# mLSTM into two gated layers, one core: set-up tiles, two-part gate rows and the order of VectorE at the start

## The chip, the cores and the metric

The program runs on one core of one Trainium2 chip. The time is device microseconds of that core, the median of three runs; "span" is the profiler's time from the first to the last instruction of one profiled execution. In the tables PE is TensorE, DVE is VectorE, ACT is ScalarE, POOL is GpSimd and SP is SyncE, whose queue issues every DMA here.

## What is computed

For 2 batches, 8 heads, 768 steps and a head size of 40, a recurrent attention with exponential gates, and then two dense layers with their own nonlinearities over the 1536 tokens of width 320:

```
m_new  = max(f + m, i);  f_stab = exp(f + m - m_new);  i_stab = exp(i - m_new)
C = f_stab*C + i_stab * v k^T;   n = f_stab*n + i_stab*k
y = sigmoid(o) * (C q) / max(|n.q|, 1)
x = y as [1536, 320]
x = (h - tanh h) @ w_out,            h = x @ w_in        (320 -> 2048 -> 320)
x = (h * tanh(softplus h)) @ w2_out, h = x @ w2_in       (320 -> 2048 -> 320)
```

## The kernel before

The recurrence is done in chunks of 128 steps. There are 12 token tiles (6 chunks of 2 batches); tile j is one `attention(j)`. The first dense layer takes tiles in blocks of two (`blk[0, k]`), so block 0 is tiles 0 and 1, and its 16 weight slices of 128 columns come in pairs: `mm1(i)` is the first product for a block and two slices, `tile1(i)` its nonlinearity, `mm2(i)` the second product. Every product that has to be precise is made from two fp32r parts, so x and each weight slice are first split in a high and a low part.

A weight slice (`conv_w`, line 166) is loaded raw and goes through three integer passes on VectorE with a scaling pass on ScalarE between the second and the third: L175, L176 (VectorE), L177 (ScalarE), L178 (VectorE, the third pass), then L179 (ScalarE, the high part) and L181 and L182 (the low part: GpSimd for the first two slices, VectorE for the others). The product `mm1(0)` needs slices 0 and 1 and x of tiles 0 and 1.

x of a tile is made at the end of `attention(j)`: products of q and k (L321), times the decay D on VectorE (L323), product with v on TensorE (L341), the denominator and two VectorE operations (L349 to L354) that write x, a copy (L141 from line 357). `transpose_x` turns it: TensorE L246, ScalarE L248 (high part), VectorE L249 (low part). D is an exponential of a sum that TensorE makes from the gate rows n and a; for chunk 0 from `n0` and `na` (L285 to L295), for later chunks from the tiles `md` and `sd` (L301), into whose rows DMAs (L269, L275) write the two-part rows `nr` of n and a.

`gates()` makes the gate rows: scans of chunk 0, their parts (`first` is the last of these, L418), and a closure `rest` that is called in steps: the scans over chunks 1 to 5 (L396 to L404), `rest_u` (L439 and the GpSimd operation L442), `rest_t` (an exponential L450, transposes and products on TensorE, the VectorE copies L454, L457 and L467) and `rest_n` (the two-part rows: two ScalarE copies L141 and two VectorE subtractions L435).

The tiles that GpSimd sets up are `cm` (L612, L613), `C` (L643), `sd` (L673, L674, L677) and `md` (L680, L683). `spin` (L592) are filler products on TensorE.

The order on each engine is made by a scheduler that takes instructions in the order in which they are traced when their inputs are expected to be ready. `after(x)` adds an edge: what is traced in it stands behind x in the queue of the engine that it shares with x. `start` holds the last instructions of `transpose_x` of tile 1 and the last L179; slices 2 and on are converted after it (`conv_to`).

## Time and profile before

| | us |
|---|---|
| runs before | 480.66, 477.70, 479.10 |
| median | 479.1 |
| profiled execution: its time | 479.02 |
| profiled execution: its span | 476.9 |
| TensorE busy in the span | 459.6 |
| VectorE, ScalarE, GpSimd busy | 320.7, 283.9, 119.5 |
| mean granted clock, share of full | 0.978 |

The profile was read on one core only, since there is one. Times of the timeline are from the span's start. A row of the timeline is: start, length, engine, line, operation, written<-read tiles, shapes, count, and in brackets the idle time of the engine just before and what ended it. Neighbouring rows of one engine may overlap by about 0.1 us, since an engine starts an instruction while the one before drains.

### The profile page before, as it was taken

To read this page: it belongs to the slowest core of one execution; us is meant where nothing else is said; L and a number is where in the kernel's file an instruction comes from. 1 tells how busy PE (TensorE), PEld (TensorE's weight loads), DVE (VectorE), ACT (ScalarE), POOL (GpSimd) and SP (SyncE) were. 2 spreads that over 40 slices of the span, in tenths; PEclk is the share of its full clock that TensorE was granted. 3 is DMA by queue.
4 is the path that set the end of the run, shared out by engine and by line. 5 is a ranking of instruction groups with operands and counts; after the bars stand their busy time and mean duration, and the time that the engine had idled before them with its cause. 6 is when DMAs were issued, how large, how long until landed. Compare 5 with 4: busy or idle time off the path is not lost.

```text
span 476.9 us, 8013 instructions
## 1 busy us (share of the span) xinstructions
PE 459.6 (96%) x3103; PEld 418.2 (88%) x3103; DVE 320.7 (67%) x544; ACT 283.9 (60%) x513; POOL 119.5 (25%) x132
## 2 busy tenths in 40 slices
PE   9868999999999999999999998999999999999996
PEld 5536898999999989999999887989989998998895
DVE  7889588998968888666899897789942321121111
ACT  3776837567576675797987675866744322332231
POOL 2912526427464252243332333100000000000000
PEclk9997959999999999999999999999999999999999
DMA  7954161542513321000101101055401000010001
GB/s 256 375 197 147 58 219 45 179 136 65 177 33 105 101 63 62 0 1 2 61 12 51 62 1 63 21 205 173 149 0 56 1 1 1 0 56 0 1 0 55
DMA packets 22745, 38.04 MB, mean 80 GB/s; under 512 B 1364, under 2 KB 17044, under 8 KB 22708
## 3 DMA queue, kind: packets, MB, share of 16 engines
q1 hardware_dynamic: 22708, 37.54, 23.8%
q8 instruction: 24, 0.39, 0.3%
q14 instruction: 13, 0.11, 0.1%
HBM read 35.41 MB, written 1.97 MB: 78 GB/s over the span
## 4 chain that ended last, share of the span: by engine, by line
PE 77%; DVE 8%; issue 5%; ACT 3%; DMA 3%; POOL 2%; ACTq 0%; DVEq 0%; POOLq 0%; SPq 0%
PE h L493 32%; PE acc L554 10%; PE acc L552 10%; PE acc L553 10%; PE sc L321 4%; PE pv L341 4%; DMA raw<-in_w_dram 3%; POOL gl L506 2%; PE it L330 2%; PE xt L246 1%; PE st L362 1%; DVE raw L176 1%; PE w_ps L592 1%; DVE g L522 1%; DVE raw L175 1%
## 5 line engine op out<-in xcount | busy, mean ns | idle before, releaser
L493 PE MATMUL h<-xT,w 128*128 128x256 f32 (+1 forms) x1152 | 212.3, 325 | 7.8 <-ACT w L179 3.4
L493 PEld LDWEIGHTS h<-xT,w 128*128 128x128 f32 x1152 | 170.8, 191 | 24.8 <-ACT w L179 4.0
L552 PE MATMUL acc<-w,gh 128*128 128x320 f32 x384 | 120.2, 315 | 1.3 <-ACT gh L141 0.8
L553 PE MATMUL acc<-w,gh 128*128 128x320 f32 x384 | 118.9, 312 | 0.0
L554 PE MATMUL acc<-w,gl 128*128 128x320 f32 x384 | 110.5, 312 | 0.1
L506 POOL TENSOR_TENSOR gl<-g,gh 128x512 fp32r<-128x512 f32 x48 | 66.5, 1386 | 137.9 <-ACT gh L141 124.0
L535 DVE TENSOR_TENSOR gl<-g,gh 128x512 fp32r<-128x512 f32 x48 | 33.1, 691 | 85.7 <-ACT g L534 85.7
L552 PEld LDWEIGHTS acc<-w,gh 128*128 128x128 f32 x384 | 73.0, 190 | 5.3 <-issue 1.3
L553 PEld LDWEIGHTS acc<-w,gh 128*128 128x128 f32 x384 | 72.8, 190 | 2.3
L533 ACT ACTIVATE gh<-h 128x512 fp32r<-128x512 f32 x48 | 28.8, 601 | 75.5 <-PE h L493 75.4
L554 PEld LDWEIGHTS acc<-w,gl 128*128 128x128 f32 x384 | 69.9, 189 | 1.8 <-POOL gl L506 0.3
L141 ACT ACTIVATE gh<-g 128x512 fp32r<-128x512 f32 x48 | 30.4, 634 | 29.8 <-DVE g L522 22.3
L522 DVE COPY_PREDICATED g<-u,t 128x512 f32<-128x512 uint32 x48 | 41.0, 855 | 7.5 <-ACT u L521 7.3
L519 DVE TENSOR_TENSOR g<-u,h 128x512 f32<-128x512 f32 x48 | 32.7, 681 | 14.7 <-ACT u L518 11.5
L521 ACT ACTIVATE u<-u,bias 128x512 f32<-128x512 f32 x48 | 34.9, 727 | 10.5 <-DVE g L519 10.4
L178 DVE SCALAR_TENSOR_TENSOR raw<-raw 128x704 uint32<-128x704 uint32 x32 | 34.5, 1082 | 7.5 <-ACT raw L177 7.3
L179 ACT ACTIVATE w<-raw 128x704 fp32r<-128x704 f32 x32 | 27.8, 875 | 16.0 <-DVE raw L178 15.9
L516 ACT ACTIVATE u<-h 128x512 f32<-128x512 f32 x48 | 28.4, 591 | 14.4 <-PE h L493 14.3
L177 ACT ACTIVATE raw<-raw 128x704 f32<-128x704 f32 x32 | 27.7, 867 | 9.3 <-DVE raw L176 8.3
L520 DVE TENSOR_TENSOR t<-h,t 128x512 f32<-128x512 f32 x48 | 32.8, 684 | 0.0
L176 DVE SCALAR_TENSOR_TENSOR raw<-raw 128x704 uint32<-128x704 uint32 x32 | 30.3, 948 | 0.3
L518 ACT ACTIVATE u<-u 128x512 f32<-128x512 f32 x48 | 30.5, 636 | 0.0
(105 smaller groups left out, 503.2 us busy)
## 6 DMA issues: line engine op xcount, KB each, us to landing
raw<-in_w_dram SPq DMA_DIRECT2D x32, 704.0 KB
qk_t<-in_qk_dram SPq DMA_DIRECT2D x12, 512.0 KB
kv_t<-in_kv_dram SPq DMA_DIRECT2D x12, 324.0 KB
out_dram<-xo SPq DMA_DIRECT2D x12, 160.0 KB
xo<-in_og_dram SPq DMA_DIRECT2D x2, 640.0 KB
xo<-in_og_dram SPq DMA_DIRECT2D x2, 320.0 KB
sd<-nr SPq DMA_DIRECT2D x20, 4.0 KB
md<-nr SPq DMA_DIRECT2D x10, 8.0 KB
```

The costliest lines, as they stand in the source:

```text
L176: nc.vector.scalar_tensor_tensor(lo32, in0=z, scalar=0x80000000, in1=lo32, op0=ALU.bitwise_and, op1=ALU.bitwise_or)
L178: nc.vector.scalar_tensor_tensor(z, in0=z, scalar=3, in1=lo32, op0=ALU.logical_shift_left, op1=ALU.bitwise_or)
L493: y = nc.tensor.matmul(t[:, k * nt:(k + 1) * nt], lhsT=w[:, o:o + P], rhs=x[:, kk, :], start=(n == 0), stop=(n == len(pairs) - 1),)
L506: nc.gpsimd.tensor_tensor(gl, in0=g, in1=gh.bitcast(F32), op=ALU.subtract)
L519: mark[:] = [nc.vector.tensor_tensor(g, in0=u, in1=h, op=ALU.mult)]
L520: nc.vector.tensor_tensor(t, in0=h, in1=t, op=ALU.subtract)
L521: nc.scalar.activation(out=u, in_=u, func=AF.Relu, bias=bias[:, 0:1])
L522: nc.vector.copy_predicated(out=g, mask=u.bitcast(U32), data=t)
L535: nc.vector.tensor_tensor(gl, in0=g, in1=gh.bitcast(F32), op=ALU.subtract)
L552: nc.tensor.matmul(a, lhsT=gh[:, sl], rhs=wh, start=(f in ends_), stop=False)
L553: nc.tensor.matmul(a, lhsT=gh[:, sl], rhs=wl, start=False, stop=False)
L554: nc.tensor.matmul(a, lhsT=gl[:, sl], rhs=wh, start=False, stop=(f + 1 in ends_ or f == NF - 1))
```

## The change

GpSimd's set-up of `sd`, `md` and `C` is traced right behind that of `cm` instead of behind the first two attentions, and the first row of `u_t` is cleared at the beginning. The steps of `rest` come in another order: the scans, `rest_n` and `rest_u` are called right after the first four steps of tile 0's attention; `rest_t` is now the one that is called after `start`. In `rest_n` the ScalarE copies stand behind the exponentials made so far, and the VectorE subtractions behind tile 0's last L323 (`scored[0]`); `rest_u`'s GpSimd operation stands behind the last `wv` (L316). For the first two weight slices the third pass (L178) of slice f stands behind the last operation on x of tile f (`gated[f]`, L354), and the first pass of slice 1 behind the third pass of slice 0.

```diff
@@ -128,6 +128,8 @@
     texp, tbl, dls = [], [], []
+    scored, gated = {}, {}
+
     spq, cvd, hold = [], [], []
     def after(x):
@@ -163,7 +165,9 @@
                     spq[:] = [x]
                 raw[layer, f] = t
-    def conv_w(layer, f):
+    third = {}
+
+    def conv_w(layer, f, first=(), behind=()):
         r = raw.pop((layer, f)).rearrange("p (n t) -> p n t", t=2)
         lo32, z = r[:, :, 0], r[:, :, 1]
         zf = z.bitcast(F32)
@@ -172,10 +176,14 @@
-        nc.vector.tensor_scalar(lo32, in0=lo32, scalar1=29, scalar2=None, op0=ALU.logical_shift_right)
+        with after(first):
+            nc.vector.tensor_scalar(lo32, in0=lo32, scalar1=29, scalar2=None, op0=ALU.logical_shift_right)
         nc.vector.scalar_tensor_tensor(lo32, in0=z, scalar=0x80000000, in1=lo32, op0=ALU.bitwise_and, op1=ALU.bitwise_or)
         scaled[layer, f] = nc.scalar.activation(out=zf, in_=zf, func=AF.Copy, scale=2.0 ** -111)
-        nc.vector.scalar_tensor_tensor(z, in0=z, scalar=3, in1=lo32, op0=ALU.logical_shift_left, op1=ALU.bitwise_or)
+        with after(behind):
+            third[layer, f] = nc.vector.scalar_tensor_tensor(
+                z, in0=z, scalar=3, in1=lo32, op0=ALU.logical_shift_left, op1=ALU.bitwise_or
+            )
         cvd[:] = [nc.scalar.activation(out=w[:, 0:WC], in_=zf, func=AF.Copy)]
         eng = nc.gpsimd if layer == 0 and f < PRE else nc.vector
         eng.tensor_tensor(w[:, WC:WT], in0=zf[:, 0:REM0], in1=wf[:, 0:REM0], op=ALU.subtract)
@@ -320,7 +328,7 @@
                 h = 4 * hf + hh
                 x = nc.tensor.matmul(sc[:, hh, :], lhsT=hp(kT, h, HP), rhs=hp(q, h, HP), start=True, stop=True)
             d4 = Dm[:, 4 * hf:4 * hf + 4, :]
-            nc.vector.tensor_tensor(d4, in0=sc, in1=d4, op=ALU.mult)
+            scored[j] = nc.vector.tensor_tensor(d4, in0=sc, in1=d4, op=ALU.mult)
             yield
         hv = ap_.tile([P, H, D1], F32, tag="hv", name="hv", bufs=2) if c else None
         hs = slice(b * H, (b + 1) * H)
@@ -351,7 +359,7 @@
         nc.vector.reciprocal(out=den, in_=den)
         x = xo[:, j, 0:DM].rearrange("p (h d) -> p h d", h=H)
         nc.vector.tensor_tensor(x, in0=hv[:, :, 0:D], in1=x, op=ALU.mult)
-        nc.vector.scalar_tensor_tensor(
+        gated[j] = nc.vector.scalar_tensor_tensor(
             x, in0=x, scalar=1 / WS, in1=den.to_broadcast([P, H, D]), op0=ALU.mult, op1=ALU.mult
         )
         copy_r(0, xo[:, j, DM:3 * P], xo[:, j, 2 * P:DM])
@@ -390,6 +398,7 @@
         nc.vector.memset(ch(rm)[:, :, 0:1], 0.0)
         nc.gpsimd.memset(na[0].bitcast(F32), 0.0)
         nc.gpsimd.memset(g_t, 0.0)
+        nc.gpsimd.memset(ch(u_t)[:, 0:1, :], 0.0)
         nc.gpsimd.tensor_tensor(sel, in0=ident[:, 0:BH], in1=ident[:, 32:32 + BH], op=ALU.add)
         def scans(a, e):
@@ -423,26 +432,29 @@
         first = parts(0)
         def rest():
-            nc.gpsimd.memset(ch(u_t)[:, 0:1, :], 0.0)
             with after([first]):
                 scans(L, S)
-            return rest_u
+            return rest_n
         def rest_n():
             for n, t in enumerate((n_t, i_t)):
                 t, hi, lo = t[:, EC * L:S], nr[64 * n:64 * n + BH], nr[64 * n + 32:64 * n + 32 + BH]
-                copy_r(0, hi, t)
-                nc.vector.tensor_tensor(lo, in0=t, in1=hi.bitcast(F32), op=ALU.subtract)
+                with after(texp):
+                    copy_r(0, hi, t)
+                with after([scored[0]]):
+                    nc.vector.tensor_tensor(lo, in0=t, in1=hi.bitcast(F32), op=ALU.subtract)
+            return rest_u
         def rest_u():
             mp = once.tile([BH, NCH, 1], F32, name="mp")
             nc.vector.tensor_tensor(
                 mp[:, 1:NCH, :], in0=ch(n_t)[:, 0:NCH - 1, L - 1:L], in1=ch(F_t)[:, 0:NCH - 1, L - 1:L], op=ALU.add
             )
-            dls[:] = [nc.gpsimd.tensor_tensor(
-                ch(u_t)[:, 1:NCH, :], in0=ch(n_t)[:, 1:NCH, :], in1=mp[:, 1:NCH, :].to_broadcast([BH, NCH - 1, L]),
-                op=ALU.subtract,
-            )]
+            with after(dls):
+                nc.gpsimd.tensor_tensor(
+                    ch(u_t)[:, 1:NCH, :], in0=ch(n_t)[:, 1:NCH, :], in1=mp[:, 1:NCH, :].to_broadcast([BH, NCH - 1, L]),
+                    op=ALU.subtract,
+                )
             return rest_t
         def rest_t():
@@ -465,7 +477,6 @@
                     rhs=ue.rearrange("p (b r g) c -> p r b g c", r=2, g=HG)[:, r], start=True, stop=True,
                 )
             nc.vector.tensor_copy(dec, d_ps)
-            return rest_n
         return rest, first
@@ -610,9 +621,31 @@
         big = cm.bitcast(F32)
         nc.gpsimd.memset(big, 0.0)
-        nc.gpsimd.affine_select(
+        masked = nc.gpsimd.affine_select(
             out=cm, in_=big, pattern=[[1, L]], base=0, channel_multiplier=-1, compare_op=ALU.is_ge, fill=2.0 ** 100
         )
+
+        for b, t in enumerate(sds):
+            f = t.bitcast(F32)
+            with after([masked]):
+                nc.gpsimd.memset(f, 0.0)
+            nc.gpsimd.affine_select(
+                out=t, in_=f, pattern=[[0, P]], base=-b, channel_multiplier=1, compare_op=ALU.not_equal, fill=1.0
+            )
+            nc.gpsimd.affine_select(
+                out=t, in_=f, pattern=[[0, P]], base=-B - b, channel_multiplier=1, compare_op=ALU.not_equal, fill=1.0
+            )
+        with after([masked]):
+            nc.gpsimd.memset(md_.bitcast(F32), 0.0)
+        mf = md_.bitcast(F32)
+        for n in range(2):
+            nc.gpsimd.affine_select(
+                out=md_, in_=mf, pattern=[[-HG, 2], [-1, HG], [0, L]], base=-K0 - H * n, channel_multiplier=1,
+                compare_op=ALU.not_equal, fill=-1.0,
+            )
+        with after([masked]):
+            for t in Cst:
+                nc.gpsimd.memset(t, 0.0)
         copy_r(0, identr, ident)
         for n, v_ in enumerate((-G_T,)):
             nc.vector.memset(bias[:, n:n + 1], v_)
@@ -634,13 +667,13 @@
                 next(g, 0)
         go(ga, 4)
+        rest = rest()
+        rest = rest()
+        rest = rest()
         go(gb, 4)
         session(0, 2)
         go(ga)
         go(gb)
-        with after(dls):
-            for t in Cst:
-                nc.gpsimd.memset(t, 0.0)
         go(ga)
         go(gb)
         loads_to(2 * B, "qk")
@@ -657,8 +690,11 @@
         def lead1(n, x=()):
             while conv1[0] < min(n, NF):
+                f = conv1[0]
                 with after(x):
-                    conv_w(0, conv1[0])
+                    conv_w(
+                        0, f, [third[0, f - 1]] if f and f < PRE else (), [gated[f]] if f < PRE else ()
+                    )
                 if conv1[0] >= PRE:
                     load_w()
                 if conv1[0] == PRE + 1:
@@ -666,29 +702,7 @@
                         load_o(*oc.pop(0))
                 conv1[0] += 1
-
-        with after(dls):
-            for b, t in enumerate(sds):
-                f = t.bitcast(F32)
-                nc.gpsimd.memset(f, 0.0)
-                nc.gpsimd.affine_select(
-                    out=t, in_=f, pattern=[[0, P]], base=-b, channel_multiplier=1, compare_op=ALU.not_equal, fill=1.0
-                )
-                nc.gpsimd.affine_select(
-                    out=t, in_=f, pattern=[[0, P]], base=-B - b, channel_multiplier=1, compare_op=ALU.not_equal, fill=1.0
-                )
-            nc.gpsimd.memset(md_.bitcast(F32), 0.0)
-            mf = md_.bitcast(F32)
-            for n in range(2):
-                nc.gpsimd.affine_select(
-                    out=md_, in_=mf, pattern=[[-HG, 2], [-1, HG], [0, L]], base=-K0 - H * n, channel_multiplier=1,
-                    compare_op=ALU.not_equal, fill=-1.0,
-                )
         spq[:] = kvd
-        lead1(1)
-        rest = rest()
-        rest = rest()
-        rest = rest()
         lead1(PRE)
         at_pools[:] = [(ps_acc, "acc")] * PS[0] + [(ps_at, "at")] * PS[2]
```

## Rows read from the trace of the kernel before

**Rows 1.** The page's head and part 1: busy us (share), xinstructions.

```profile
span 476.9 us, 8013 instructions
...
PE 459.6 (96%) x3103; PEld 418.2 (88%) x3103; DVE 320.7 (67%) x544; ACT 283.9 (60%) x513; POOL 119.5 (25%) x132
```

**Rows 2.** Windows view: stretch, length, busy PE PEld DVE ACT POOL, PEclk, DMA share, GB/s.

```profile
30.50:34.10 3.60, 0.69 (x3) 0.10 (x1) 3.56 (x6) 3.60 (x7) 0.00 (x0) 1.00 0.04 11
...
35.70:42.50 6.80, 5.37 (x19) 4.04 (x20) 6.68 (x9) 3.09 (x5) 1.28 (x1) 0.50 0.11 30
...
59.60:73.20 13.60, 13.60 (x82) 12.65 (x81) 11.59 (x31) 4.62 (x9) 2.76 (x3) 0.50 0.63 196
73.20:240.00 166.80, 166.26 (x1333) 159.68 (x1333) 136.52 (x232) 119.40 (x232) 70.88 (x71) 1.00 0.23 73
```

**Rows 3.** Timeline of VectorE, 7 to 27 us (columns as told above).

```profile
7.61 1.54 DVE L404 TENSOR_TENSOR_SCAN n_all<-gg,n_all,gi 16x640 f32<-16x640 f32 x1
...
12.53 0.53 DVE L175 TENSOR_SCALAR raw<-raw 128x704 uint32<-128x704 uint32 x1 [1.72 <-DMA raw<-in_w_dram]
13.09 1.30 DVE L176 SCALAR_TENSOR_TENSOR raw<-raw 128x704 uint32<-128x704 uint32 x1
14.31 1.27 DVE L323 TENSOR_TENSOR Dm<-sc,Dm 128x512 f32<-128x512 f32 x2
17.23 1.91 DVE L178 SCALAR_TENSOR_TENSOR raw<-raw 128x704 uint32<-128x704 uint32 x1 [1.64 <-ACT raw L177]
...
21.22 1.03 DVE L354 SCALAR_TENSOR_TENSOR xo<-xo,den 128x320 f32<-128x320 f32 x1
...
23.83 0.62 DVE L457 TENSOR_TENSOR ue<-ident,gu 16x96 f32<-16x96 f32 x1
24.38 0.47 DVE L354 SCALAR_TENSOR_TENSOR xo<-xo,den 128x320 f32<-128x320 f32 x1
...
26.37 0.25 DVE L454 COPY uT<-u_ps 128x96 f32<-128x96 f32 x1
26.54 0.20 DVE L467 COPY dec<-d_ps 128x48 f32<-128x48 f32 x1
```

**Rows 4.** Timeline of TensorE: tile 1's product with v, the first product.

```profile
15.91 1.98 PE L341 MATMUL pv<-kv_t,Dm 128*128 128x41 f32 x16
...
27.29 1.25 PE L493 MATMUL h<-xT,w 128*128 128x256 f32 x8
```

**Rows 5.** Raw weight tile, 0 to 50 us: ns min/median/max, first and last start, forms.

```profile
L176 DVE SCALAR_TENSOR_TENSOR raw<-raw x7: 890/894/1306, 13.1 to 47.2; 128x704 uint32<-128x704 uint32 x7
...
L178 DVE SCALAR_TENSOR_TENSOR raw<-raw x6: 885/982/1947, 17.2 to 40.8; 128x704 uint32<-128x704 uint32 x6
L179 ACT ACTIVATE w<-raw x6: 850/853/864, 19.2 to 42.7; 128x704 fp32r<-128x704 f32 x6
...
L181 POOL TENSOR_TENSOR w<-raw,w x2: 1432/1612/1793, 20.1 to 25.4; 128x576 fp32r<-128x576 f32 x2
L182 POOL TENSOR_TENSOR w<-raw,w x2: 462/529/596, 22.0 to 26.9; 64x128 fp32r<-64x128 f32 x2
```

**Rows 6.** Timeline of GpSimd, 14 to 18 us.

```profile
14.50 0.95 POOL L680 MEMSET md<- 128x1024 f32 x1
...
15.41 0.55 POOL L674 TENSOR_SCALAR_AFFINE_SELECT sd<-sd 128x128 fp32r<-128x128 f32 x2
...
15.93 1.09 POOL L683 TENSOR_SCALAR_AFFINE_SELECT md<-md 128x1024 fp32r<-128x1024 f32 x1
...
17.14 1.25 POOL L442 TENSOR_TENSOR gu<-n_all,mp 16x640 f32<-16x640 f32 x1
```

**Rows 7.** Timeline of ScalarE and VectorE: an exponential, the two-part rows.

```profile
10.76 0.60 ACT L304 ACTIVATE Dm<-nb 128x512 f32<-128x512 f32 x1 [1.86 <-PE nb L295]
...
26.82 0.72 ACT L141 ACTIVATE nr<-n_all 16x640 fp32r<-16x640 f32 x1
...
28.41 0.81 DVE L435 TENSOR_TENSOR nr<-n_all,nr 16x640 fp32r<-16x640 f32 x1
```

## The prediction

> **What bounds the kernel now.** I read the page first. TensorE is busy for 459.6 of 476.9 us [rows 1], and from 73 us on it has hardly a gap: 166.26 us of 166.80 in the stretch up to 240 us, at the full granted clock [rows 2]. There it is the bound, and nothing in the change touches that work. What the change can move is the time at which this dense work begins, and what happens until 73 us. So I went on to the windows and then to the timeline of the first 45 us.
>
> The timeline shows the first product of the dense layer, `mm1(0)`, at 27.29 us [rows 4]. All that stands before it on TensorE is attention for two tiles and filler. It needs x of tiles 0 and 1 and weight slices 0 and 1, and both come through VectorE. Between the landing of slice 0 (L175 at 12.53) and the end of the last operation on x (L354, 24.38 + 0.47 = 24.85) VectorE has 12.32 us, and the reader is to see in [rows 3] how they go: an idle wait of 1.64 for the scaling pass, a third pass of 1.91, a second pass of 1.30, an L354 of 1.03 where the other took 0.47, and an L457 that x does not need. From 30.5 to 34.1 us VectorE and ScalarE are full (3.56 and 3.60 of 3.60) and TensorE works 0.69 us [rows 2]: the conversions of slices 2 and 3 are then the bound. So a gain at the start is a gain of VectorE's queue, up to the point where TensorE takes over.
>
> **The change part by part.** The sum is made against the profiled execution, 479.02 us (span 476.9 [rows 1], 2.1 us around it); the median of the three runs, 479.1, is as good as the same.
>
> *x ahead of the third passes.* Taken off the 12.32 us: the idle 1.64 before L178, which x of tile 0 can now fill, as its product with v is ready before that of tile 1; the third pass of slice 1, which now stands behind x of tile 1, 0.89 at its shortest [rows 5]; and L457, 0.62, which goes behind `start` [rows 3]. Together 3.15 us.
>
> *The set-up tiles taken away from here.* Three VectorE instructions are long beside GpSimd work: L178 took 1.91 where the shortest took 0.89 [rows 3, 5], so 1.02; L354 1.03 against 0.47, so 0.56 [rows 3]; L176 1.30 against 0.89 [rows 3, 5], so 0.41. The first ran beside GpSimd's L442 (17.14 to 18.39) [rows 6], and behind that the set-up selects; with the selects gone, and L442 traced early, GpSimd is free there until slice 0's low part. I take back 1.99 us. L354's part is the least sure, since L181 on GpSimd (shortest 1.43) remains and may meet another VectorE operation instead.
>
> Together 5.14: x of tile 1 ends at 24.85 - 5.14 = 19.7 us. Its product with v ends at 15.91 + 1.98 = 17.89 [rows 4], which leaves 1.8 us for its five small VectorE operations, so TensorE does not forbid it. From there to `mm1(0)` it was 27.29 - 24.85 = 2.44 us (copy, transposes, L248), which I keep; so `mm1(0)` could start at 22.15, 5.1 us earlier. Is slice 0 ready? Its third pass comes right behind x of tile 0, ending at about 17.9 (19.7 less the 1.8 us of tile 1's operations); L179 0.85, L181 1.43 and L182 0.46 [rows 5] end at 20.6. So it is, by 1.5 us. Slice 1's third pass is late next: behind x of tile 1, it ends at about 21 to 22, and its low part 2.7 us later, at 24 to 25, while the first half of `mm1(0)` runs; before, both slices were ready at 27.4.
>
> *rest_n moved to the front.* Two VectorE subtractions of 0.81 and two ScalarE copies of 0.72 (one row of each stands in [rows 7]) leave the full stretch after 27 us. In front VectorE idles 1.72 us ahead of L175, waiting for the weights' DMA [rows 3], which takes the pair of 1.63; ScalarE idles 1.86 us ahead of tile 1's exponentials at 10.76 [rows 7], which takes the copies of 1.45. If that cover is gone they cost themselves: 1.6 us on VectorE. On ScalarE, what is queued behind the copies is tile 1's exponentials, the table loads and the sigmoid, and L177, for which L178 waits. *rest_t* goes the other way: 0.62 + 0.25 + 0.20 = 1.07 us of VectorE [rows 3] and an exponential on ScalarE come behind `start`; its users come with chunk 1, some 30 us later. Behind `start`, then, VectorE has 1.63 less and 1.07 more, and the third pass of slice 1 (0.89) stands there too: what was moved cancels, and the gain for slices 2 and 3 is the idle time, the three collisions and the subtractions, 1.64 + 1.99 + 1.63 = 5.3 us. Both ways of counting give just over 5.
>
> *DMAs.* No load changes its place in SP's queue. The DMAs of `nr` into `md` and `sd` are issued as early as their rows are ready, but the chunk-1 products that need them come much later; I cost them at nothing. Later weight loads wait for a free raw buffer, that is for the conversions, and come earlier with them.
>
> *The set-up tiles at their new place.* This speaks against the change, and the trace has no row of these selects beside the scans. GpSimd has nothing to do between `cm` and tile 0's `wv`; VectorE runs the gate scans until 7.61 + 1.54 = 9.15 us [rows 3]. The selects take 4 x 0.28 (a pair is 0.55) and 2 x 1.09, 3.3 us, the large memset 0.95 [rows 6]. From below the cost is nothing: GpSimd does them while VectorE's operations happen not to collide. From above it is all of them, 3.3 + 0.95 = 4.3 us, if VectorE waits for each. The nearest row is that L178 which lost 1.02 beside one GpSimd read. VectorE's only slack is the 1.72 us before L175, and the subtractions take nearly all of that. I take one long collision and one short one, 1.2 us.
>
> The Trainium skill, page "SBUF — State Buffer", section "Who interferes with whom", says that a VectorE instruction with two SBUF inputs contends with a GpSimd instruction that reads SBUF, not with one that only writes it, and that the one that started first holds the shared pair for its whole length. The trace agrees so far: L178 (two inputs in SBUF) lost 1.02 us beside L442, while the pair of L323 (one input in PSUM) took 1.27 beside the memset of `md` [rows 3, 6]. By that rule alone the memset costs nothing, and the six selects cost up to 3.3.
>
> Sum: 5.1 - 1.2 = 3.9 us earlier, and 479.02 - 3.9 = **475.1 us**.
>
> **The rivals.** *Collisions at the front eat it.* The scans read two SBUF inputs, as L178 does, and every select reads; if VectorE gets the pair last each time, the scans end 3.3 to 4.3 us later, the subtractions lose their cover, tile 0's L323 stands behind the scans, and the gain is 5.1 - 4.3 = 0.8: 478.2 us. For it speaks the 1.02 us of L178; against it, that most set-up is short. The page's rule named above is this mechanism with 3.3 us, which would give 477.2. Chance 17%.
>
> *The gain is given back at slices 2 and 3, or the order on VectorE hardly changes.* `mm1(0)` starts early, but VectorE's total work before 45 us hardly falls, L181 on GpSimd meets other VectorE operations, and `mm1(1)` starts about where it did. Only the subtractions less `rest_t` would stay, 1.63 - 1.07 = 0.6: 478.4 us. For it: VectorE is full there [rows 2]. Against it: 3.6 us of idle time and collisions are real time of that same queue. Chance 12%.
>
> *The granted clock does better.* Twice it is 0.50: from 35.7 to 42.5, after TensorE had worked 0.69 of 3.60 us, and from 59.6 to 73.2 [rows 2]. With the subtractions gone from the conversions TensorE waits less, and the first drop may not come: half of 6.8, 3.4 us, gives 471.7. Chance 13%.
>
> *The granted clock does worse, and the kernel is slower.* The same wait for slices 2 and 3 comes at another time, as does the session of sigmoids before 59.6; if there is one more low stretch as long as the second, 13.6 us with TensorE busy throughout [rows 2], it costs half, 6.8 us: 475.1 + 6.8 = 481.9. It decides from 7.8 us of additional half clock on, where it has eaten the 3.9. For it: both low stretches stand in the part that is being shifted. Against it: the shift makes TensorE's waits shorter, not longer. Chance 10%.
>
> **How the numbers follow.** The forecast has 48%, the rivals 17, 12, 13 and 10. The forecast's own range is 473.8 (no collision, gain 5.2) to 476.5. The range of all is 471.5 to 479.0: it takes in the two cases with a small gain and the better clock, and leaves out the worse clock and what lies beyond. About 1% (4.8 us) is what a measurement of this kernel can tell from no change, so faster means below 474.3: the better clock, 13%, and about half of the forecast, 25%: 38%. Slower by over 1% means over 483.9, the upper half of the worse clock: 6%. The rest, 56%, is within 1%.
>
> **What would show it.** Right: `mm1(0)` at 22 to 24.5 us; both L354 done before 21 us, at 0.47; L178 of slice 0 at 0.89; the subtractions between 10 and 14 us; scans that end between 9.2 and 10.5; the first product of slice 2, which before ended the stretch at 34.1 [rows 2], at about 30. Wrong in the first way: scans that end after 12 us, with L404 or L399 far longer than before. Wrong in the second: `mm1(0)` early and that first product of slice 2 still after 33. The clock cases show in the length of the two low stretches. What would make the whole prediction wrong is another order on VectorE after `start`, or a wait on ScalarE of which the rows tell nothing, as the copies and the exponential were moved between one another.

## The result and the profile after

The changed kernel takes 475.25 us (median of 20 runs, 472.4 to 476.74); the kernel before took 479.21, measured beside it (20 runs). The ratio is 0.9917, 95% interval 0.9895 to 0.9939: faster by 0.8%, 4.0 us. Forecast were 475.1 and a range of 471.5 to 479.0. Ratios, and the medians of the versions below, leave out runs that lie over 1.5% above the fastest of their kernel: one of the kernel before here, three of ten for the order of rest alone, five of twelve for `rest_t` alone.

The page of the changed kernel, its head and part 1 (busy us, share, xinstructions), as in [rows 1]:

```profile
span 474.5 us, 8023 instructions
...
PE 459.5 (97%) x3103; PEld 416.8 (88%) x3103; DVE 323.9 (68%) x544; ACT 284.1 (60%) x513; POOL 123.8 (26%) x132
```

The profiled execution is only 2.4 us shorter than that of before, at the same TensorE work; its own time, 476.55 us, is among the longest of the 20. Line numbers have moved: L312 was L304, L331 was L323, L349 was L341, L362 was L354, L180, L181, L182 and L184 were L175, L176, L177 and L178, L410, L412 and L413 were L401, L403 and L404, L427 was L418, L445 was L435, L504 was L493, and the ScalarE copy L143 was L141; on GpSimd L639, L642 and L648 were L680, L683 and L643, and L189 was L181.

The timeline of the changed kernel, VectorE, ScalarE, GpSimd and TensorE up to the first product of slice 2:

```profile
3.27 0.96 POOL L639 MEMSET md<- 128x1024 f32 x1
...
3.74 1.19 DVE L410 TENSOR_SCALAR n<-gi 16x128 fp32r<-16x128 f32 x1
...
4.17 0.69 POOL L648 MEMSET C<- 128x328 f32 x2
...
5.39 1.09 POOL L642 TENSOR_SCALAR_AFFINE_SELECT md<-md 128x1024 fp32r<-128x1024 f32 x1
5.56 1.06 DVE L427 TENSOR_TENSOR n<-n_all,n 32x128 fp32r<-32x128 f32 x1
...
8.19 1.75 POOL L642 TENSOR_SCALAR_AFFINE_SELECT md<-md 128x1024 fp32r<-128x1024 f32 x1
...
8.90 1.05 DVE L412 COPY gg<-gF 16x5 f32<-16x5 f32 x1
...
9.99 1.54 DVE L413 TENSOR_TENSOR_SCAN n_all<-gg,n_all,gi 16x640 f32<-16x640 f32 x1
...
11.56 0.74 ACT L143 ACTIVATE nr<-n_all 16x640 fp32r<-16x640 f32 x1 [1.80 <-DVE n_all L413]
...
12.01 1.27 DVE L331 TENSOR_TENSOR Dm<-sc,Dm 128x512 f32<-128x512 f32 x2
...
13.08 1.09 ACT L312 ACTIVATE Dm<-nb 128x512 f32<-128x512 f32 x2
...
13.31 0.81 DVE L445 TENSOR_TENSOR nr<-n_all,nr 16x640 fp32r<-16x640 f32 x1
...
15.01 0.53 DVE L180 TENSOR_SCALAR raw<-raw 128x704 uint32<-128x704 uint32 x1
...
18.27 0.83 ACT L182 ACTIVATE raw<-raw 128x704 f32<-128x704 f32 x1
...
18.35 0.49 DVE L362 SCALAR_TENSOR_TENSOR xo<-xo,den 128x320 f32<-128x320 f32 x1
...
19.13 0.89 DVE L184 SCALAR_TENSOR_TENSOR raw<-raw 128x704 uint32<-128x704 uint32 x1 [0.28 <-ACT raw L182]
...
21.02 1.66 POOL L189 TENSOR_TENSOR w<-raw,w 128x576 fp32r<-128x576 f32 x1 [4.89 <-ACT w L187]
...
22.01 1.03 DVE L362 SCALAR_TENSOR_TENSOR xo<-xo,den 128x320 f32<-128x320 f32 x1
...
25.41 1.56 PE L504 MATMUL h<-xT,w 128*128 128x256 f32 x8 [0.43 <-ACT xT L256]
...
32.66 0.73 PE L504 MATMUL h<-xT,w 128*128 128x256 f32 x4 [2.13 <-ACT w L187]
```

Read from the top. Three small VectorE operations stand beside GpSimd's set-up and take 1.19, 1.06 and 1.05 us; in the trace of before they took 0.22, 0.28 and 0.15. L410 ends only after the memsets, L427 and L412 end after a select of `md`. That is 2.65 us, and the scans end at 9.99 + 1.54 = 11.53 instead of 9.15 [rows 3]. Both engines pass the delay on: VectorE comes to the first pass of slice 0 (L180) at 15.01 instead of 12.53, and on ScalarE the copies of the two-part rows wait 1.80 us for the scans and hold tile 1's exponentials (L312) until 13.08, where they were at 10.76 [rows 7]. The weight side is what the forecast wanted: the third pass of slice 0 at 0.89 instead of 1.91, behind x of tile 0. The first product starts at 25.41 instead of 27.29 [rows 4], the first product of slice 2 at 32.66 instead of 34.1. These are single executions.

Windows of the changed kernel on its low stretches of the clock and behind them (stretch, length, busy PE, PEld, DVE, ACT, POOL, granted clock, DMA share, GB/s):

```profile
34.10:40.90 6.80, 5.11 (x19) 3.77 (x19) 6.68 (x11) 3.67 (x6) 0.55 (x1) 0.50 0.16 33
58.00:68.20 10.20, 10.20 (x58) 9.89 (x57) 8.58 (x20) 3.81 (x8) 4.92 (x6) 0.50 0.55 164
68.20:240.00 171.80, 171.45 (x1381) 163.83 (x1380) 141.60 (x239) 122.81 (x238) 73.21 (x71) 1.00 0.23 71
```

Both low stretches of [rows 2] are there again, the first as long as before, the second 10.2 us instead of 13.6. From 68 us on TensorE is the bound, as before from 73 us.

### The profile page after: what moved, and what is told of

Its sections match the earlier page's. It is cut to its first block, busy times and chain, and to the rows that moved or that the text cites. A ratio compares the mean times of both kernels' runs of the same rounds, so it can differ in the third digit from the quotient of the medians.

```text
span 474.5 us, 8023 instructions
## 1 busy us (share of the span) xinstructions
PE 459.5 (97%) x3103; PEld 416.8 (88%) x3103; DVE 323.9 (68%) x544; ACT 284.1 (60%) x513; POOL 123.8 (26%) x132
## 4 chain that ended last, share of the span: by engine, by line
PE 66%; issue 4%; DVE 3%; POOL 2%; DMA 2%; ACT 0%; ACTq 0%; DVEq 0%; POOLq 0%; SPq 0%
PE h L504 29%; PE acc L563 10%; PE acc L564 10%; PE acc L565 9%; PE sc L329 3%; PE pv L349 2%; POOL gl L517 2%; DMA raw<-in_w_dram 2%; PE it L338 1%; PE xt L254 1%; DVE g L533 1%; DVE t L531 1%; DVE g L530 1%; PE st L370 1%; PE nb L309 0%
## 5 line engine op out<-in xcount | busy, mean ns | idle before, releaser
L504 PE MATMUL h<-xT,w 128*128 128x256 f32 (+1 forms) x1152 | 211.6, 325 | 7.0 <-DVE w L189 2.4
L504 PEld LDWEIGHTS h<-xT,w 128*128 128x128 f32 x1152 | 169.8, 191 | 23.9 <-DVE w L189 2.6
L517 POOL TENSOR_TENSOR gl<-g,gh 128x512 fp32r<-128x512 f32 x48 | 64.8, 1351 | 152.3 <-ACT gh L143 142.1
L143 ACT ACTIVATE gh<-g 128x512 fp32r<-128x512 f32 x48 | 30.4, 634 | 29.3 <-DVE g L533 25.2
L527 ACT ACTIVATE u<-h 128x512 f32<-128x512 f32 x48 | 28.3, 590 | 10.9 <-PE h L504 10.6
L182 ACT ACTIVATE raw<-raw 128x704 f32<-128x704 f32 x32 | 27.5, 862 | 12.2 <-DVE raw L181 10.5
L184 DVE SCALAR_TENSOR_TENSOR raw<-raw 128x704 uint32<-128x704 uint32 x32 | 30.7, 965 | 3.6 <-ACT raw L182 3.4
L181 DVE SCALAR_TENSOR_TENSOR raw<-raw 128x704 uint32<-128x704 uint32 x32 | 31.0, 972 | 0.3
```

What stands on the lines that cost most here:

```text
L181: nc.vector.scalar_tensor_tensor(lo32, in0=z, scalar=0x80000000, in1=lo32, op0=ALU.bitwise_and, op1=ALU.bitwise_or)
L184: third[layer, f] = nc.vector.scalar_tensor_tensor(z, in0=z, scalar=3, in1=lo32, op0=ALU.logical_shift_left, op1=ALU.bitwise_or)
L504: y = nc.tensor.matmul(t[:, k * nt:(k + 1) * nt], lhsT=w[:, o:o + P], rhs=x[:, kk, :], start=(n == 0), stop=(n == len(pairs) - 1),)
L517: nc.gpsimd.tensor_tensor(gl, in0=g, in1=gh.bitcast(F32), op=ALU.subtract)
```

## The experiments

The theory is called A: VectorE's queue up to the first products sets the time, and every part of the change works through it. Its rivals are B, that the two-part rows leaving the conversions carry the gain, and C, that the granted clock does. All medians stand beside the kernel before, measured on the same chip at the same time: 479.41 us for the versions `e1` to `e4`, 479.98 for `e5` to `e8`, 479.53 for `e9` to `e12`; each stands at the head of its experiment. A difference between two versions of different groups is taken between their distances from the kernel before. The granted clock has two levels here, 1.00 and 0.50 of full speed, so the half-clock time of a run is twice (1 - mean granted clock) times its span.

### The set-up alone

`e1`. To the kernel before, the new place of the set-up and nothing else:

```diff
+        nc.gpsimd.memset(ch(u_t)[:, 0:1, :], 0.0)
...
+        for b, t in enumerate(sds):
+            f = t.bitcast(F32)
+            with after([masked]):
+                nc.gpsimd.memset(f, 0.0)
...
-        with after(dls):
-            for b, t in enumerate(sds):
...
```

> The kernel before with only GpSimd's set-up tiles moved to the beginning. Theory A (VectorE's queue up to the first product decides, and the set-up selects cost about as much beside the early scans as they cost beside the weight passes): scans end at about 11.5 us as in the changed kernel, L178 of slice 0 falls from 1.91 to about 0.9 us, first product between 25.5 and 27.3, 1 us faster than before or less. Theory B (the gain comes from the two-part rows leaving the stretch after the first product): no change, within 0.5 us of before. Theory C (the low stretches of the granted clock decide): the time follows the half-clock time, whatever the first product does.

Measured: 479.44 us, ratio 0.9998 (0.9975 to 1.0022). No gain, as both A (1 us or less) and B allowed; but the first product of its profile is at 29.9 us, later than before, which no theory expected. The section on the one edge, below, shows what held it.

### All but the set-up

`e2`. To the changed kernel, the set-up put back:

```diff
-            with after([masked]):
-                nc.gpsimd.memset(f, 0.0)
...
+        with after(dls):
+            for t in Cst:
+                nc.gpsimd.memset(t, 0.0)
...
+        with after(dls):
+            for b, t in enumerate(sds):
...
```

> The changed kernel with GpSimd's set-up tiles in their old place and the rest of the change kept. Theory A: scans end at 9.2 us again, third passes are long again (1.9 us once, or L354 at 1.0), first product at 24.5 to 26, time within 1 us of the changed kernel, so 3 to 5 us faster than before. Theory B: as the changed kernel, 4 us faster than before. If the set-up's new place carries the gain instead, the time is within 1 us of before.

Measured: 476.09 us, ratio 0.9947 (0.9921 to 0.9973). That is 3.3 us faster than before by the medians, so the set-up is not needed for most of the gain. In its profile, one of its longer executions (478.13 us), the scans end at 9.2 us again, but the first pass of slice 0 takes 2.92 us beside the set-up in its old place (0.53 in the kernel before), TensorE's clock was half from 19.3 to 26.1 us, and the first product was at 28.3, outside the 24.5 to 26 of theory A and later than before.

### The set-up made by ScalarE

`e3`. To the changed kernel, in place of the memsets and selects of `sd` and `md` (`cols` holds sums of two groups of columns of the identity, made by two GpSimd operations):

```diff
+        for b, t in enumerate(sds):
+            nc.scalar.activation(out=t, in_=cols[:, b:b + 1].to_broadcast([P, P]), func=AF.Copy)
+        nc.scalar.activation(
+            out=md_, in_=cols[:, B:B + H].rearrange("p (r g o) -> p r g o", r=2, o=1).to_broadcast([P, 2, HG, L]),
+            func=AF.Copy, scale=-1.0,
+        )
```

> The changed kernel, but sd and md are made from two small column sums of the identity by GpSimd and spread by three ScalarE copies in its idle time before 7 us; no large memset of md, no select. Theory A: VectorE meets no GpSimd read in the scans: the first set of scans ends at 5.2 us, all scans at 9.2 to 9.5 instead of 11.5; first product 1.5 to 2.4 us earlier than in the changed kernel, at 23 to 24 us; 6 us faster than before. Theory B: no faster than the changed kernel. Theory C: follows the half-clock time only.

Measured: 473.85 us, ratio 0.9885 (0.9861 to 0.9908), 5.6 us faster than before, where the changed kernel was 4.0; the intervals of the two ratios overlap a little, so "better than the changed kernel" is likely and not settled. Its timeline:

```profile
3.32 0.51 ACT L636 ACTIVATE sd<-cols 128x128 fp32r<-128x128 f32 x2 [0.83 <-POOL cols L632]
3.71 0.43 DVE L410 TENSOR_SCALAR n<-gi 16x128 fp32r<-16x128 f32 x1
3.73 1.04 ACT L637 ACTIVATE md<-cols 128x1024 fp32r<-128x1024 f32 x1
...
7.43 0.15 DVE L412 COPY gg<-gF 16x5 f32<-16x5 f32 x1
7.62 1.54 DVE L413 TENSOR_TENSOR_SCAN n_all<-gg,n_all,gi 16x640 f32<-16x640 f32 x1
...
24.56 1.56 PE L504 MATMUL h<-xT,w 128*128 128x256 f32 x8 [0.18 <-ACT xT L256]
```

The three ScalarE copies take 1.55 us in an idle stretch, L412 is back at 0.15, L410 takes 0.43 (0.22 in the kernel before), and the scans end at 9.16. So the collisions at the front are real and cost 2.4 us of VectorE's queue; of the time they cost about 1.6 us by the two distances, 5.6 and 4.0, which is not settled either. A's expectation of the scans held; the first product came 0.9 us earlier, not 1.5 to 2.4. The rest goes to other waits: tile 0's L331 now waits 0.89 us for TensorE's scores, and the two third passes wait 0.60 and 0.53 for ScalarE.

### The old order of rest, and one edge on GpSimd

`e4`. To the changed kernel, the old order and place of rest's steps, without the edges in them:

```diff
         go(ga, 4)
-        rest = rest()
-        rest = rest()
-        rest = rest()
...
+        lead1(1)
+        rest = rest()
+        rest = rest()
+        rest = rest()
         lead1(PRE)
```

> The changed kernel with the steps of rest in the order and place of before (rest_n behind start, rest_t early); set-up early and x ahead of the third passes are kept. Theory A: first product no later than in the changed kernel (25.4) or up to 1 us earlier, as the front of VectorE has 1.6 us less; but the conversions of slices 2 and 3 lose 1.6 us, so 0.5 to 1.5 us slower than the changed kernel, 2.5 to 3.5 faster than before. Theory B: all of the gain is gone, within 1 us of before.

Measured: 479.31 us, ratio 0.9987 (0.9958 to 1.0016): all of the gain is gone. By these numbers B had won. The timeline, then the windows, show something else:

```profile
11.80 1.25 POOL L450 TENSOR_TENSOR gu<-n_all,mp 16x640 f32<-16x640 f32 x1 [1.87 <-DVE mp L447]
...
13.02 0.19 POOL L147 TENSOR_SCALAR dl<-Dm 128x8 f32<-128x8 f32 x1
...
13.25 1.29 DVE L331 TENSOR_TENSOR Dm<-sc,Dm 128x512 f32<-128x512 f32 x2 [1.53 <-POOL dl L147]
...
14.04 1.95 PE L349 MATMUL pv<-kv_t,Dm 128*128 128x41 f32 x16 [0.36 <-issue]
...
17.19 3.64 PE L349 MATMUL pv<-kv_t,Dm 128*128 128x41 f32 x16
```

```profile
12.00:16.00 4.00, 3.64 (x34) 3.43 (x34) 2.72 (x4) 3.88 (x5) 2.86 (x5) 1.00 1.10 354
16.00:20.00 4.00, 4.00 (x20) 3.19 (x20) 3.83 (x11) 2.59 (x5) 0.00 (x0) 0.51 1.10 347
```

GpSimd's L450 (L442 before) stands ahead of tile 0's `dl` in its queue and waits for the late scans. `dl` reads the last column of D, which L331 overwrites, so L331 waits 1.53 us, the product with v comes late, TensorE idles 0.36 us, and then its clock is at half from 16 us on: tile 1's product with v takes 3.64 us instead of 1.98. The same wait of 1.53 us, and half clock from 15 us on, stand in the trace of `e1`. The new order of rest has an edge that puts this GpSimd operation behind `wv`. The next kernel, `e11`, adds that edge alone to the one above:

```diff
-            dls[:] = [nc.gpsimd.tensor_tensor(
+            with after(dls):
+                nc.gpsimd.tensor_tensor(
...
```

> The changed kernel with the old order of rest (which came out as before), plus one edge: GpSimd's operation of rest_u stands behind both wv. There the trace had tile 0's L331 at 13.25 us waiting 1.53 for GpSimd's copy dl, which stood behind that operation, which waited for the scans. If this wait is what cost that version its gain: L331 starts at about 11.7 to 12.1 again, the product with v about 1 us earlier, TensorE does not idle between 13 and 14 us, no low clock from 16 us on, 1 to 3 us faster than without the edge. If rest_t in the front is what cost it: within 0.7 us of that version.

Measured: 475.59 us, ratio 0.9926 (0.9899 to 0.9953), 3.9 us faster than before, where the same kernel without the edge was 0.1: 3.8 us for the edge, more than the 1 to 3 expected. Its timeline and its window:

```profile
9.91 0.20 POOL L147 TENSOR_SCALAR dl<-Dm 128x8 f32<-128x8 f32 x1
...
12.01 1.27 DVE L331 TENSOR_TENSOR Dm<-sc,Dm 128x512 f32<-128x512 f32 x2
...
13.52 1.53 POOL L451 TENSOR_TENSOR gu<-n_all,mp 16x640 f32<-16x640 f32 x1
...
25.27 1.56 PE L502 MATMUL h<-xT,w 128*128 128x256 f32 x8 [0.46 <-ACT xT L256]
```

```profile
16.00:20.00 4.00, 3.72 (x52) 2.96 (x51) 3.47 (x10) 2.43 (x6) 0.00 (x0) 1.00 1.12 359
```

`dl` is at 9.91, L331 without a wait, the clock at 1.00, the first product at 25.27. With the set-up early and x first, this one edge is worth as much as the whole new order of rest; that is shown. What it saves is not late scans alone: in `e6` and `e10` below, which lack the edge too, the scans end at 9.2 us, and the GpSimd operation is still ahead of `dl` (at 9.45 and 9.41 us) and tile 0's L331 still waits 1.53. There the clock does not fall at 16 us, so the wait alone does not bring the low clock.

### Rest's order alone, and its two halves alone

`e5`. To the kernel before, the new order of rest with its edges:

```diff
         go(ga, 4)
+        rest = rest()
+        rest = rest()
+        rest = rest()
...
-        lead1(1)
-        rest = rest()
-        rest = rest()
-        rest = rest()
         lead1(PRE)
```

> The kernel before with only the new order of rest's steps. Set-up alone and set-up with x ahead of the third passes both came out as before, so rest's order is in every version that gained. Theory B2 (rest's order alone carries it: the subtractions leave the stretch after the first product): 2 to 4 us faster than before. Theory A2 (the parts only work together: x ahead of the third passes shortens the front, and rest's order keeps that gain from being lost at slices 2 and 3): within 1 us of before.

Measured: 475.26 us against 479.98, 4.7 us faster; ratio 0.9889 (0.9856 to 0.9922), its runs spread from 471.2 to 478.6. Order alone gives as much as the whole change. That the subtractions carry it, as B2 has it, is not shown by this: `rest_t` and the edge moved with them. First product 26.1, first product of slice 2 at 32.4.

`e9`. To the kernel before, only `rest_t` moved; `rest()()` calls `rest_t` and then `rest_n`:

```diff
         rest = rest()
         rest = rest()
-        rest = rest()
...
         with after(start):
-            rest()
+            rest()()
```

> The kernel before with only rest_t moved: its exponential, transposes and three VectorE copies come behind start, where rest_n stays too. Theory T (rest_t held up the front: its ScalarE exponential and its products stand ahead of the work on x, and it is worth most of the 3 to 4 us that the new order of rest alone gave): first product at about 26, 2 to 3.5 us faster than before. Theory N (the two-part rows leaving the conversions are worth it): within 1 us of before.

Measured: ratio 0.997 (0.9935 to 1.0005), median 477.07 us; the median of all twelve is 479.64. Six took 475.6 to 477.7 us with 10 to 22 us of half clock, six 481.6 to 484.5 with 29 to 32. In its profile, one of the first six, the clock was half from 18.1 to 24.9 us and the first product at 28.3, not about 26. So theory T is not borne out, and not refuted for the runs whose clock held.

`e10`. To the kernel before, only `rest_n` moved, with its edges:

```diff
         go(ga, 4)
+        rest = rest()
+        rest = rest()
...
-        with after(start):
-            rest()
```

> The kernel before with only rest_n moved to the front, into the idle times of VectorE and ScalarE; rest_t stays in the front. Theory T: within 1.2 us of before, as 1.6 us less behind start is bought with a fuller front. Theory N: 2 to 3.5 us faster than before.

Measured: 477.1 us, ratio 0.9959 (0.9937 to 0.9981), 2.4 us faster, as theory N expected. Its first product is at 27.15, hardly earlier than before, and its first product of slice 2 at 33.48, 0.6 us earlier; it carries the wait of 1.53 us for `dl`. The same part within the change is weighed by `e7`, the changed kernel with only `rest_n` put back behind `start`:

```diff
         rest = rest()
         rest = rest()
-        rest = rest()
...
         with after(start):
-            rest()
+            rest()()
```

> The changed kernel with only the two-part rows (rest_n: two ScalarE copies, two VectorE subtractions) back behind start, as the last step; rest_t stays behind start too, so VectorE has 1.63 us more there than in the changed kernel. If the subtractions carry the gain: 1.5 to 3 us slower than the changed kernel. If it is rest_t that had to leave the front (its exponential on ScalarE, its transposes on TensorE and 1.07 us on VectorE, which stood ahead of x's transposes): within 1 us of the changed kernel.

Measured: 476.35 us against 479.98, ratio 0.9936 (0.9909 to 0.9964), 3.6 us faster than before; the changed kernel was 4.0. Within the change the subtractions are worth 0.4 us, which cannot be told from nothing. That is the second case of the expectation, but it does not make `rest_t` the carrier: `e11`, with `rest_t` in front and the edge kept, was 3.9 us faster than before. Its first product is at 23.56, 1.9 us earlier than in the changed kernel, and its first product of slice 2 at 31.93:

```profile
10.79 0.60 ACT L312 ACTIVATE Dm<-nb 128x512 f32<-128x512 f32 x1 [1.86 <-PE nb L303]
...
16.37 0.84 ACT L182 ACTIVATE raw<-raw 128x704 f32<-128x704 f32 x1
...
23.56 1.56 PE L502 MATMUL h<-xT,w 128*128 128x256 f32 x8 [0.20 <-ACT xT L256]
...
31.93 0.89 PE L502 MATMUL h<-xT,w 128*128 128x256 f32 x4 [3.25 <-ACT w L187]
```

So in the changed kernel the two-part rows cost 1.9 us of the front: once the scans end at 11.5, the idle time that was to cover them is gone. ScalarE shows the same 1.9: without the copies tile 1's exponentials start at 10.79 instead of 13.08, and L182, for which the third pass waits, at 16.37 instead of 18.27. Whether the copies or VectorE's subtractions count for more is not separated. Behind the front the rows give it back, as `e7` then waits longer for its conversions: its lead is 0.7 us at the first product of slice 2 and gone at the next wait (35.84 against 35.79).

Four versions with the set-up early and x first, then, differ only in rest. With its old order they are 0.1 us faster than before (`e4`), with the edge 3.9 (`e11`), with the edge and `rest_t` behind `start` 3.6 (`e7`), and with `rest_n` in front as well 4.0 (the changed kernel). Of the order of rest, the edge is the part that is shown to count there. It takes away a wait that the kernel before does not have.

### x ahead of the third passes, alone and with a clear front

`e6`. To the kernel before (the first row of `u_t` is cleared at the beginning here too):

```diff
-                    conv_w(0, conv1[0])
+                    conv_w(
+                        0, f, [third[0, f - 1]] if f and f < PRE else (), [gated[f]] if f < PRE else ()
+                    )
```

> The kernel before with only x of the first two tiles ahead of the weight slices' third passes. Theory B2: no change. Theory A2: no change either or 1 us faster. If it is 2 us or more faster, set-up at the beginning is what cost the version with both its gain.

Measured: 477.91 us, ratio 0.9961 (0.9942 to 0.998), 2.1 us faster, first product at 26.3. B2 expected no change and A2 at most 1 us. Its wait of 1.53 us for `dl` is told above.

`e12`. To the version with the set-up by ScalarE:

```diff
-                    conv_w(
-                        0, f, [third[0, f - 1]] if f and f < PRE else (), [gated[f]] if f < PRE else ()
-                    )
+                    conv_w(0, f)
```

> The version whose set-up is spread by ScalarE, without the edges that put x of the first two tiles ahead of the third passes; the new order of rest is kept. If x ahead of the third passes is worth something once the front is clear: 1 us or more slower than that version (which was 5.6 us faster than before). If not: within 0.7 us of it, 5 to 6 us faster than before.

Measured: 476.51 us against 479.53, ratio 0.9934 (0.9909 to 0.9959): 3.0 us faster than before, where the version with the edges was 5.6. The edges are worth about 2.1 alone and 2.5 in the clear front. How they do it there is open: in the two profiles the first product is only 0.2 us earlier with them (24.56 against 24.75), and the first product of slice 2 is 0.8 later (31.83 against 31.03). Beside the set-up in its old place and the new order of rest they add nothing (3.3 us with them in `e2`, 4.7 without in `e5`).

### Filler in TensorE's wait

`e8`. To `mm1` of the version with the set-up by ScalarE:

```diff
+                if i == 1 and k == 0 and n == 3:
+                    keep(8, y)
-                keep(3, y)
+                keep(9 if i == 0 and k else 3, y)
```

> The version whose set-up is spread by ScalarE, with 14 more filler products in TensorE's two waits for slice 2 (behind mm1(0) and in the middle of mm1(1)'s first half), about 1.3 and 1.7 us of work in waits of 2.1 and 2.4 us. Theory of the clock (a low stretch costs about a quarter to a half of its length): the first low stretch, 6.8 us from about 34 us on, is gone, and the time is 1.5 to 3.4 us below that version. Rival (that stretch stands where TensorE waits for VectorE anyway and costs nothing): no change, or slower by what the filler delays.

Measured: 475.44 us against 479.98, ratio 0.9908 (0.9886 to 0.9931). The windows of this kernel:

```profile
33.80:40.60 6.80, 6.43 (x35) 4.03 (x32) 6.64 (x10) 4.38 (x8) 1.79 (x1) 1.00 0.32 106
51.00:64.70 13.70, 13.70 (x75) 13.29 (x74) 10.65 (x21) 5.69 (x10) 5.64 (x6) 0.50 0.55 184
```

The first low stretch is gone, as intended, and a long one stands at 51 us; over its four runs the half-clock time is 14.0 us on average, as good as the 14.9 of the six without filler. It is 1.1 us slower relative to before than that version (4.5 against 5.6), with intervals that overlap. Low clock was moved, not removed, so the price of the first stretch stays open.

## Why the prediction came out right, and where its steps did not

**The total.** 475.1 was forecast, 475.25 measured, and that they agree so well is in part luck: the path to it held less well than the sum. The front gave 1.9 us in the profiled execution, not 3.9: the first product is at 25.41, outside the 22 to 24.5 that were named, x of tile 1 ends at 23.04, not 19.7, and the first product of slice 2 is at 32.66, not 30. The span is 2.4 us shorter. The medians differ by 4.0. On VectorE the 1.9 can be followed. L180 starts 2.48 us late (15.01 against 12.53), where the forecast allowed 1.2: the scans are 2.38 late and the subtractions take 1.63, and the idle 1.72 that was to take them is gone, which makes 2.3 of it. From there to the end of tile 1's x it is 8.03 us instead of 12.32, so 4.29 were saved of the 5.14; what is missing is a second L362 of 1.03 and a wait of 0.28. 4.29 less 2.48 is 1.81, where the forecast had 5.1 less 1.2.

**Where the rest of the median comes from.** Over the 20 runs of the changed kernel the time goes with the half-clock time: correlation 0.88, 0.21 us per us of half clock; the seven runs with under 12 us of it have a median of 473.5, the eight with over 20 a median of 475.7. The runs of before in the experiments had 21.0 us on average (80 runs), those of the changed kernel 16.6. At 0.21 the difference is 0.9 us. But the 80 runs of before show only 0.09 us per us (correlation 0.26), which makes it 0.4, and the ten of `e5` show 0.49, so there is no one price. What is left of the 4.0, 3.1 to 3.6 us, is more than the 1.9 and 1.4 us that the two first products came earlier in the profiles; where the rest lies is not shown. These are correlations over undirected runs; the one attempt to force it, the filler, did not decide it. Over the fourteen profiled executions (before, changed and the twelve versions) the span goes with the start of the first product of slice 2 (correlation 0.83) more than with the half-clock time (0.70); the two are not independent of each other (0.59), so A is favoured over C and not shown against it. The clock rivals of the prediction priced a low stretch at half its length; the runs of the changed kernel show about a fifth.

**x ahead of the third passes: right, but for 0.28 us.** x of tile 0 filled the wait for ScalarE, the third pass of slice 0 took 0.89, the idle time before it fell from 1.64 to 0.28. Alone it was worth 2.1 us, with the wait for `dl` in it.

**The set-up taken away from the weight passes: 1.4 of 1.99 us.** L178 gave back its 1.02 us and L176 0.42 (0.88 instead of 1.30), though L176 had stood beside `wv` as well as the set-up in the kernel before (`wv` from 12.62 to 13.64 us), and `wv` stays. The collision of L354 only moved: the first gave back 0.54, the second took 1.03, beside L189 on GpSimd (21.02 to 22.68). The prediction had named this as the least sure.

**The set-up at its new place: the term was mis-sized.** It was put at 1.2 us between 0 and 4.3; the scans end 2.38 us later. Of the total the collisions cost about 1.6 us by the version without the selects and the memset of `md`, which its interval does not settle. The mechanism was the one named, but the memsets were judged by the wrong clause: L410, with one input, waited out the memsets of `md` and `C`. That is not the case of two SBUF inputs. The Trainium skill, page "SBUF — State Buffer", section "Who interferes with whom", has another clause for it, that copies, casts and `tensor_scalar` can, under conditions on their operands, run in a two-port mode and then contend with GpSimd; L410 (0.22 to 1.19 us) and L412 (0.15 to 1.05 us for five columns) agree with it. L427 (0.28 to 1.06 us), with two inputs beside a select, fits the clause that the prediction used.

**rest_n into idle time, rest_t behind start: right in one order of things, nothing in the other.** Moved alone, rest_n gave 2.4 us (1.63 forecast). Within the change it gave 0.4: the prediction saw that the cover of 1.72 us had no slack left and that collisions would come on top, and yet counted the subtractions as a full gain behind `start`. With the cover gone it priced VectorE's 1.6 us and, for ScalarE, only listed what is queued behind the copies; that queue came 1.9 us later (L182 at 18.27, and at 16.37 with rest_n behind `start`). rest_t alone gave nothing that could be told.

**The step that was overlooked.** The prediction says of GpSimd only that L442 is "traced early" and that it is free. The edge that puts it behind `wv` decides over 3.8 us with the set-up early: `dl` must not stand behind it, or L331 waits. It was in the diff, and no cost was given to it. In the kernel before, `dl` is at 8.98 us and L442 at 17.14, behind the set-up and the clearing of the first row of `u_t` (16.97), so the trace of before could not show this wait; that GpSimd's queue order against `dl` had to be followed, it could. The four traces that have the wait (`e1`, `e4`, `e6`, `e10`) all clear that row before 3 us; whether that is what lets the operation come first, no run shows by itself.

**Two of the chances do not follow from the ranges.** "Faster" was to begin below 474.3, which is a fifth of the way into the forecast's own 473.8 to 476.5, so about 9 of its 48% lie there, not 25. "Slower" was to begin above 483.9, which lies above the 481.9 of the worse clock, so it is not that case's upper half.

**Parts that do not add.** The set-up alone gave 0, x first alone 2.1, rest's order alone 4.7, the three together 4.0. Set-up alone and x first alone lack the edge and carry the wait for `dl`, so neither was seen without it; the two together with the edge, and rest in its old order, give 3.9 (`e11`). So there are two ways to about 4 us, one without rest's new order and one with nothing else, and both together give no more. That they draw on the same few us before the first product is the likely reason, not a shown one.

## What to carry to other kernels

Set-up work that is moved to an "idle" GpSimd at the beginning was not free here, with VectorE on the path: give it to an engine beside which VectorE's operations keep their length (here three ScalarE copies of 1.55 us in place of 4.6 us of memsets and selects), and follow what is queued behind it. When one operation in an engine's queue gets a late input, look for the small one behind it that releases something else; an edge that swaps the two can be worth more than the work that was moved. Parts that shorten the same wait are to be tried one by one and together, since their gains need not add; and a part tried alone is to be read in its own trace, as it can bring a wait that the whole change does not have.

## What the runs showed of the hardware

A five-column VectorE copy took 1.05 us instead of 0.15 beside a GpSimd select of 1024 columns, and a VectorE `tensor_scalar` on 16 x 128 took 1.19 instead of 0.22 beside the memsets of `md` and `C`. In `e4` TensorE's granted clock fell to half at 16 us after it had worked 3.64 us of the 4 before; in `e11`, one edge more, it worked all 4 of them and 3.72 of the next 4, and the clock stayed at 1.00 through both. Two rows make no rule. From one run to the next the changed kernel spends between 7 and 24 us at half clock, and its time moves by 4 us with that.
